# One attention-and-GLU kernel: its order of work planned with reserves, and one TensorE semaphore for two

## The chip, the core and the metric

The kernel runs on one core of one Trainium2 chip. The metric is the time of one execution on the device in microseconds (us), as the median of several runs. The core has five engines that take instructions in order from queues of their own and meet only through semaphores: TensorE (PE in the profile; its weight loads are PEld), VectorE (DVE), ScalarE (ACT), GpSimd (POOL) and SyncE (SP, which here only issues DMAs).

## The reference

`x` has 2048 tokens of 512 features, in bf16. The result mixes two branches by a gate per token:

```python
g = sigmoid((x * gate_w).sum(-1, keepdims=True))
qkv = x @ wqkv                      # 32 heads of 16
p = softmax(q @ k.T / 4)            # per head, 2048 x 2048
a = (p @ v) @ wo
b = ((x @ w_gate) * (x @ w_up)) @ w_down      # 1376 hidden
out = g * a + (1 - g) * b
```

## The kernel before

**The attention.** 32 heads in 4 stretches of 512 queries are handled as 32 *quads*: a quad is four heads (one of 8 sets) for one stretch `c` of queries (`quad`, line 187). For a quad the keys come in 16 tiles of 128; one key tile of one quad is a *step*, so there are 512 steps. A step has four score products of 128 keys by 512 queries, each into one PSUM bank. The exponential of the four banks is taken in one of two ways:

- an A step by ScalarE: `exp` (line 1709) reads one bank, or two neighbouring banks at once, and writes bf16 cells in whatever buffers are free (PT, and hT, wd, wu, wg, wo, xT while they aren't needed for themselves);
- a D step by VectorE: `dpass` (line 1747) adds a constant, clips, and writes int16 whose bits are an approximate exponential. `copy` (line 1756), on VectorE or GpSimd, makes three shifted copies, so that TensorE can sum four approximations (buffers DB, wv, wk). Only key tiles 2, 4, 7, 9, 12 and 14 may be D steps; whichever of them the planner doesn't give to VectorE falls to ScalarE.

Then V products add up the quad's output in PSUM bank 7. When the 16 steps of a quad are in, `o_copy` (line 1828) takes it out and its softmax sums go through DRAM for the division.

**The fill.** All other products (K, Q, V, gate, up, down, output projection) are *units* of a list that `setup` writes; a unit takes one bank, and VectorE empties it.

**The two halves.** TensorE is used as two halves of 64 rows, `r` = 0 and 1. `pe64` (line 1616) issues one product as four matmuls on four column groups of one half; a unit runs its first part in one half and the second in the other. Seven PSUM banks (0 to 6) are shared among A products, D products and fill.

**What sets the order.** Nothing is in loops: `_Sched` plays the kernel through on the host, before it is built, with durations for each engine, and every decision of this play writes the next instruction of an engine's queue. So its durations and thresholds decide only the order of the instructions on each engine; on the chip each waits for what it needs. The lines that matter:

- `s_a` (line 305) and `s_d` (line 333) issue a score product for ScalarE or VectorE and note when it is ready for it: `t = self.now + 0.385 + 0.056`.
- `try_act` counts an exponential as 0.833 ns a column and 0.051 us; the bank is free 0.12 + 0.05 us after that. `dve_pass` counts a pass as 0.065 us and 0.533 us a bank, and 0.083 us more to its end.
- `try_pe` and `pe_phase` choose the next product. The thresholds are tables in `PAR`, one value for each of 180 windows of 4 us of planned time, written as (count, value). Among them: `alook`, `alook2` (exponential products that may stand unread), `amax`, `dmax`, `fmax` (banks of A, D and fill), `skew` (lead of one half), `dact` (open D steps), `dl` (most D steps of a quad), `dend` (with fewer steps left than this in the current quad, no more D steps of it), `fstart` (units in their first part), `ghalf`, `gfull` (VectorE's backlog from which GpSimd takes copies), `cpmax`.

**Waits.** `_Plan.op` gives each operation a *stream*, which is one semaphore; products of half `r` have stream `pe0` or `pe1`. `_Plan.emit` (line 48) leaves out a wait that the engine knows to be met already, by an earlier wait on the same stream or by what the awaited operation itself had waited for; products of the same half don't wait for each other, since TensorE runs in order. For each stream that is left the greatest count is waited for by a `wait_ge` (line 82). An instruction carries one wait; a further one is an instruction of its own on the queue, which the profile has under L82.

Of the kernel before, what the change touches and what calls it, by code (L numbers as in the profile page):

```python
# [15 lines left out]
class _Op:  # L16
    __slots__ = ("eng", "fn", "deps", "stream", "inc", "seq", "count", "waits", "needed", "know")

    def __init__(self, eng, fn, deps, stream, inc):
        self.eng = eng  # L20
        self.fn = fn
        self.deps = deps
        self.stream = stream
        self.inc = inc
        self.seq = 0
        self.count = 0
        self.waits = []
# [109 lines left out]
class _Sched:  # L137
# [167 lines left out]
    def s_a(self, r):  # L305
# [20 lines left out]
        t = self.now + 0.385 + 0.056  # L326
# [6 lines left out]
    def s_d(self, r):  # L333
# [22 lines left out]
        t = self.now + 0.385 + 0.056  # L356
# [363 lines left out]
    def try_act(self):  # L720
# [51 lines left out]
        dur = 0.833e-3 * 512 * n + 0.051  # L772
# [10 lines left out]
        t = self.now + dur + 0.12 + 0.05  # L783
# [75 lines left out]
    def dve_pass(self, now):  # L859
# [9 lines left out]
        if self.dready and self.dready[0][0] <= now and (mate or not hold):  # L869
# [12 lines left out]
            dur = 0.065 + 0.533 * n  # L882
# [4 lines left out]
            t = self.now + dur + 0.083  # L887
# [661 lines left out]
class _Hw:  # L1549
# [66 lines left out]
    def pe64(self, r, mms, deps):  # L1616
        def fn(pe):
            o = None
            for dst, lhs, rhs, st, sp, cc in mms:
                o = pe.matmul(dst, lhs, rhs, start=st, stop=sp, tile_position=(64 * r, 32 * cc), skip_group_check=True)  # L1620
            return o

        return self.P.op("pe", fn, deps, "pe%d" % r)
# [302 lines left out]
    def prologue(self):  # L1926
# [119 lines left out]
        if self.par["acc"]:  # L2046
# [14 lines left out]
 'alook': ((13, 2), (5, 6), (8, 4), (6, 2), (9, 4), (3, 5), (21, 2), (3, 3), (3, 2), (1, 4), (5, 2), (18, 5),  # L2061
# [4 lines left out]
 'amax': ((7, 5), (35, 4), (6, 5), (81, 4), (6, 5), (45, 4)),  # L2066
 'amin': ((7, 3), (6, 2), (13, 4), (6, 2), (9, 3), (3, 2), (6, 4), (2, 2), (22, 3), (28, 4), (5, 3), (18, 4),
          (7, 3), (5, 4), (5, 2), (19, 4), (5, 3), (5, 4), (9, 3)),
 'apick': ((38, 0), (6, 1), (3, 0), (6, 1), (2, 0), (2, 1), (4, 0), (12, 1), (1, 0), (12, 1), (5, 0), (1, 1),
           (5, 0), (14, 1), (11, 0), (25, 1), (14, 0), (6, 1), (13, 0)),  # L2070
 'ares': ((5, 1), (6, 2), (3, 1), (21, 2), (3, 1), (6, 2), (7, 1), (1, 2), (8, 1), (17, 2), (15, 1), (6, 0),
          (24, 2), (9, 1), (9, 0), (22, 2), (18, 1)),
 'await': ((2, 0.05), (10, 0), (6, 0.05), (5, 0), (6, 0.2), (3, 0), (3, 0.2), (3, 0.1), (3, 0.2), (3, 0),
           (7, 0.05), (1, 0.2), (8, 0.05), (11, 0), (3, 0.2), (6, 0), (3, 0.4), (6, 0.05), (3, 0.1), (10, 0),
           (5, 0.4), (4, 0.2), (10, 0.05), (1, 0.4), (3, 0), (15, 0.05), (2, 0.2), (19, 0.05), (3, 0.4),
           (8, 0), (8, 0.2)),
 'cpmax': ((2, 10), (9, 6), (24, 8), (3, 5), (6, 8), (11, 2), (5, 3), (11, 6), (1, 5), (10, 10), (17, 14),
           (3, 2), (19, 8), (1, 14), (5, 6), (6, 14), (2, 10), (5, 5), (22, 8), (12, 3), (6, 8)),
 'dact': ((13, 2), (13, 3), (18, 2), (16, 3), (12, 2), (30, 3), (19, 2), (4, 3), (22, 2), (14, 3), (1, 2),
          (12, 3), (6, 2)),  # L2080
 'dahead': ((7, 0), (34, 1), (14, 0), (35, 1), (3, 0), (4, 1), (5, 0), (59, 1), (10, 0), (9, 1)),
# [13 lines left out]
 'dpair': ((17, 1), (6, 2), (3, 0), (15, 1), (14, 0), (13, 1), (6, 2), (9, 0), (4, 2), (7, 0), (1, 2), (2, 1),  # L2095
           (5, 2), (9, 0), (10, 1), (10, 0), (6, 1), (10, 0), (18, 1), (1, 0), (14, 1)),
 'dpri': ((13, 1), (31, 0), (20, 1), (1, 0), (6, 1), (26, 0), (5, 1), (40, 0), (5, 1), (25, 0), (8, 1)),
 'dresv': ((67, 0), (7, 1), (7, 2), (99, 0)),
 'dwait': ((2, 0.4), (11, 0), (5, 0.2), (5, 0.4), (3, 0.1), (12, 0.2), (6, 0), (7, 0.2), (1, 0), (8, 0.2),
           (11, 0.4), (3, 0.2), (9, 0.4), (6, 0.2), (8, 0.1), (14, 0), (10, 0.2), (21, 0.4), (5, 0),  # L2100
           (14, 0.2), (6, 0.1), (3, 0), (1, 0.1), (9, 0)),
 'fcf': ((7, 1), (34, 0), (3, 1), (136, 0)),
 'fdebt': ((2, 0), (12, -10), (12, 25), (6, -30), (9, 0), (1, -30), (6, 0), (12, -10), (5, 25), (6, -30),
           (3, 0), (9, 25), (3, 10), (9, 0), (7, 25), (9, 0), (10, 10), (8, 25), (6, 0), (2, 10), (5, -10),
           (5, 10), (14, 25), (5, 0), (1, 10), (3, -10), (10, 10)),
 'ffn0': 2.6,
 'ffn1': 31.5,
 'flead': ((2, 160), (3, 0), (15, 80), (3, 160), (15, 80), (6, 160), (7, 20), (1, 160), (8, 20), (2, 80),
           (9, 10), (6, 80), (15, 160), (10, 10), (5, 40), (4, 160), (18, 80), (5, 20), (3, 0), (3, 20),
           (7, 160), (14, 80), (13, 40), (6, 80)),  # L2110
 'fmax': ((18, 3), (8, 2), (18, 3), (6, 2), (21, 1), (12, 2), (9, 3), (10, 1), (19, 3), (1, 2), (5, 3),
          (10, 2), (43, 3)),
 'fres': ((44, 0), (16, 2), (29, 0), (13, 2), (28, 0), (2, 2), (10, 1), (38, 0)),
 'fs2': ((13, 1), (22, 0), (3, 1), (6, 0), (20, 1), (10, 0), (6, 1), (3, 0), (6, 1), (3, 0), (9, 1), (20, 0),
         (4, 1), (10, 0), (5, 1), (22, 0), (18, 1)),
# [108 lines left out]
```

## Time and profile before

| what | value |
|---|---|
| median of 3 runs | 709.44 us (707.34 to 713.36) |
| profiled execution | 708.04 us; its span, first to last instruction, 706.3 us |
| granted TensorE clock | 1.00 |
| SyncE's DMA queue, q1 | 18.86 MB, 11.1% of the 16 DMA engines |
| HBM | 11.71 MB read, 2.36 MB written |

A row of the groups reads: line, engine, operation, output<-input by the names of the buffers, shapes, count, then busy us and mean ns of one, then the idle time of the engine ahead of these instructions and what ended it. A row of the waits reads: engine, what it was about to write, line, what it waited for, then us in total, times, and the longest. In a row of a line's own view three durations stand for the least, the median and the greatest in ns. Only waits of 0.15 us and more are listed; shorter gaps count as the pipeline's own. PEld's rows stand for TensorE's queue, since a product starts with its weight load.

### The profile page before, as it was taken

The numbers are of one execution on the slowest core, as the hardware profiler recorded it, in microseconds if no ns is written. First come the engines' busy times: TensorE is split into PE (matmuls) and PEld (weight loads), VectorE is DVE, ScalarE is ACT, GpSimd is POOL, SyncE is SP. The second block draws the span as 40 slices with busy tenths as digits, with TensorE's granted clock in tenths as the row PEclk, the third lists the DMA queues.
The fourth block names the chain that finished last, engine by engine and source line by source line (L and its number), as shares of the span: only waits on it lengthen the run. The fifth ranks groups of instructions, "written<-read, shape, count | busy, mean of one in ns | idle before, by whom it ended". The sixth has DMA issues, their size and how long they took to land.

```text
span 706.3 us, 47734 instructions
## 1 busy us (share of the span) xinstructions
PE 692.3 (98%) x22103; PEld 358.7 (51%) x22103; DVE 645.9 (91%) x1060; ACT 684.8 (97%) x820; POOL 450.7 (64%) x351
## 2 busy tenths in 40 slices
PE   8999999999999999999999999999999999999997
PEld 4564555554444545554554445555553555555553
DVE  5999999899999999999998998999999978989985
ACT  6899999999999999999999999999999999999994
POOL 3365658877464666655675747777666788487630
PEclk9999999999999999999999999999999999999999
DMA  9202341003010100001000010100001010000101
GB/s 156 69 6 57 78 107 36 6 20 94 16 35 5 35 18 23 28 11 28 13 23 23 15 33 19 36 13 13 27 7 40 12 36 24 14 23 18 29 19 33
DMA packets 33752, 22.97 MB, mean 33 GB/s; under 512 B 19500, under 2 KB 30156, under 8 KB 33552
## 3 DMA queue, kind: packets, MB, share of 16 engines
q1 hardware_dynamic: 32416, 18.86, 11.1%
q8 instruction: 173, 2.83, 1.6%
q0 software_dynamic: 176, 0.53, 0.3%
q10 hardware_dynamic: 960, 0.52, 0.3%
q14 instruction: 27, 0.22, 0.1%
HBM read 11.71 MB, written 2.36 MB: 20 GB/s over the span
## 4 chain that ended last, share of the span: by engine, by line
PE 90%; DVE 3%; ACT 3%; issue 1%; DMA 1%; ACTq 0%; DVEq 0%
PE ps L1620 90%; DVE DB L1754 2%; ACT xT L1718 1%; ACT PT L1718 1%; DVE DB L1760 1%; DMA DB<-in_A_x_dram 1%; ACT wu L1718 0%; DVE wv L1754 0%; DVE oc L1830 0%; DVE hT L1902 0%; PE ps L2017 0%; ACTq L1933 0%; DVE wu L1813 0%; ACT wd L1718 0%; ACT QM L2030 0%
## 5 line engine op out<-in xcount | busy, mean ns | idle before, releaser
L1620 PE MATMUL ps<-QM,KT 64*32 64x512 bf16 x8192 | 496.6, 379 | 4.2 <-issue 1.3
L1764 POOL TENSOR_TENSOR DB<-DB,cadd 128x512 int32<-128x512 int32 (+1 forms) x207 | 280.2, 1373 | 146.9 <-DVE DB L1760 62.0
L1718 ACT ACTIVATE PT<-ps 128x1024 bf16<-128x1024 f32 (+1 forms) x394 | 358.5, 1016 | 1.6 <-PE ps L1620 0.7
L1754 DVE TENSOR_SCALAR DB<-ps 128x512 int16<-128x512 f32 (+1 forms) x493 | 327.7, 692 | 31.8 <-PE ps L1620 28.3
L1620 PE MATMUL ps<-DB,Vs 64*17 64x512 bf16 x2856 | 261.6, 377 | 0.7
L1718 ACT ACTIVATE xT<-ps 128x1024 bf16<-128x1024 f32 (+1 forms) x270 | 258.6, 1043 | 1.9 <-PE ps L1620 1.7
L1620 PEld LDWEIGHTS ps<-QM,KT 64*32 64x32 bf16 x8192 | 152.2, 89 | 177.9 <-ACT PT L1718 46.9
L1620 PE MATMUL ps<-PT,Vp 64*17 64x512 bf16 x1444 | 204.5, 376 | 0.3 <-issue 0.2
L1620 PE MATMUL ps<-xT,Vp 64*17 64x512 bf16 x1030 | 165.3, 376 | 0.2
L1620 PE MATMUL ps<-xT,wu 64*32 64x512 bf16 x1376 | 111.9, 377 | 0.0
L1620 PE MATMUL ps<-xT,wg 64*32 64x512 bf16 x1376 | 110.5, 377 | 1.0 <-issue 0.9
L1760 DVE TENSOR_SCALAR DB<-DB 128x2048 int16<-128x2048 int16 (+1 forms) x160 | 107.3, 701 | 0.6 <-PE ps L1620 0.2
L1620 PE MATMUL ps<-wd,hT 64*32 64x512 bf16 x1408 | 100.2, 377 | 0.1
L1620 PE MATMUL ps<-DB,Vp 64*17 64x512 bf16 x1000 | 97.0, 377 | 0.6 <-DVE oc L1830 0.2
L1620 PEld LDWEIGHTS ps<-DB,Vs 64*17 64x17 bf16 x2856 | 70.6, 87 | 37.0 <-PE ps L1620 10.5
L1718 ACT ACTIVATE wd<-ps 128x1024 bf16<-128x1024 f32 (+1 forms) x69 | 65.7, 1059 | 0.6 <-PE ps L1620 0.4
L1764 POOL TENSOR_TENSOR DB<-wv,cadd 128x512 int32<-128x512 int32 (+1 forms) x38 | 49.7, 1331 | 24.2 <-DVE wv L1754 9.6
L1620 PEld LDWEIGHTS ps<-PT,Vp 64*17 64x17 bf16 x1444 | 51.2, 87 | 17.9 <-PE ps L1620 4.6
L1764 POOL TENSOR_TENSOR wv<-DB,cadd 128x512 int32<-128x512 int32 (+1 forms) x31 | 42.1, 1371 | 19.7 <-DVE DB L1760 7.8
L1754 DVE TENSOR_SCALAR wv<-ps 128x512 int16<-128x512 f32 x72 | 47.6, 683 | 2.5 <-PE ps L1620 2.1
L1764 POOL TENSOR_TENSOR wk<-DB,cadd 128x512 int32<-128x512 int32 (+1 forms) x30 | 39.4, 1324 | 15.8 <-DVE DB L1760 11.2
L1620 PEld LDWEIGHTS ps<-xT,Vp 64*17 64x17 bf16 x1030 | 40.8, 87 | 11.6 <-PE ps L1620 2.6
(108 smaller groups left out, 839.5 us busy)
## 6 DMA issues: line engine op xcount, KB each, us to landing
rb<-rscr SPq DMA_DIRECT2D x16, 256.0 KB
QM<-qraw SPq DMA_DIRECT2D x124, 16.0 KB, 2.3
oc<-oraw SPq DMA_DIRECT2D x60, 32.0 KB, 2.2
out_dram<-ost SPq DMA_DIRECT2D x12, 128.0 KB, 1.7
wd<-in_B_w_down_dram SPq DMA_DIRECT2D x10, 128.0 KB, 2.5
wu<-in_B_w_up_dram SPq DMA_DIRECT2D x12, 96.0 KB, 2.2
wg<-in_B_w_gate_dram SPq DMA_DIRECT2D x12, 96.0 KB, 2.6
wv<-in_A_wqkv_dram POOLq DMA_DIRECT2D x1, 512.0 KB, 5.2
```

The source lines that it names most:

```text
L1620: o = pe.matmul(dst, lhs, rhs, start=st, stop=sp, tile_position=(64 * r, 32 * cc), skip_group_check=True)
L1718: return self.P.op("act", lambda a: a.activation(dst, src, ACT.Exp, scale=self.ES), deps)
L1754: return self.dve(lambda v: v.tensor_scalar(dst, src, self.YB, 0.0, ALU.add, ALU.max), deps)
L1760: return self.dve(lambda e: e.tensor_scalar(o, a, 32.0 * v, None, ALU.add), deps)
L1764: lambda e: e.tensor_tensor(o.bitcast(I32), a.bitcast(I32), self.cadd[:, v, :].bitcast(I32).to_broadcast([128, n]), ALU.add),
```

## The change

1. Each operation of TensorE by `pe64` goes to one stream, `pe`, so both halves count on one semaphore. A new field `half` keeps what was left out before: products of the same half don't wait for each other.
2. The planner counts a score product as ready later, by 0.09 us for ScalarE (`mga`) and by 0.06 us for VectorE (`mgd`).
3. The planner's fixed parts move: ScalarE 0.051 to 0.055 us (and 0.12 to 0.116 after it), VectorE 0.065 to 0.069 (and 0.083 to 0.079 after it).
4. The tables of thresholds in `PAR` are other ones, 36 of them, and with them the order of the work on all engines. Formats, sizes, buffers, the computation and the number of D key tiles allowed stay.

The diff, cut to its core; of the tables those that the prediction names:

```diff
 class _Op:
-    __slots__ = ("eng", "fn", "deps", "stream", "inc", "seq", "count", "waits", "needed", "know")
+    __slots__ = ("eng", "fn", "deps", "stream", "inc", "seq", "count", "waits", "needed", "know", "half")
...
+        self.half = None
...
-                if d.eng == "pe" and o.eng == "pe" and d.stream == o.stream:
+                if d.eng == "pe" and o.eng == "pe" and d.half == o.half:
                     continue
...
-        t = self.now + 0.385 + 0.056
+        t = self.now + 0.385 + 0.056 + self.par["mga"]
         self.cnt += 1
         heapq.heappush(self.aready, (t, self.cnt, e, ci, bank, op))
...
-        t = self.now + 0.385 + 0.056
+        t = self.now + 0.385 + 0.056 + self.par["mgd"]
         self.cnt += 1
         heapq.heappush(self.dready, (t, self.cnt, e, ci, bank, op))
...
-        dur = 0.833e-3 * 512 * n + 0.051
+        dur = 0.833e-3 * 512 * n + 0.055
...
-        t = self.now + dur + 0.12 + 0.05
+        t = self.now + dur + 0.116 + 0.05
...
-            dur = 0.065 + 0.533 * n
+            dur = 0.069 + 0.533 * n
...
-            t = self.now + dur + 0.083
+            t = self.now + dur + 0.079
...
-        return self.P.op("pe", fn, deps, "pe%d" % r)
+        o = self.P.op("pe", fn, deps)
+        o.half = r
+        return o
...
- 'alook2': ((18, 4), (5, 3), (9, 0), (6, 2), (3, 0), (3, 3), (3, 0), (5, 5), (1, 3), (2, 0), (5, 6), (11, 3),
-            (3, 5), (9, 3), (6, 2), (6, 6), (6, 5), (1, 4), (29, 0), (4, 6), (5, 2), (7, 0), (10, 4), (10, 0),
-            (13, 4)),
- 'amax': ((7, 5), (35, 4), (6, 5), (81, 4), (6, 5), (45, 4)),
+ 'alook2': ((8, 4), (5, 3), (1, 4), (3, 6), (1, 4), (5, 3), (9, 0), (5, 5), (21, 4), (10, 6), (10, 4), (2, 3),
+            (3, 0), (8, 4), (1, 6), (3, 5), (9, 6), (6, 4), (18, 5), (21, 4), (6, 5), (9, 0), (16, 6)),
+ 'amax': ((7, 5), (157, 4), (6, 5), (10, 4)),
...
- 'dact': ((13, 2), (13, 3), (18, 2), (16, 3), (12, 2), (30, 3), (19, 2), (4, 3), (22, 2), (14, 3), (1, 2),
-          (12, 3), (6, 2)),
+ 'dact': ((13, 2), (24, 3), (4, 2), (3, 3), (14, 2), (79, 3), (8, 2), (19, 3), (6, 1), (10, 3)),
...
- 'dend': ((2, 2), (3, 3), (2, 1), (10, 0), (6, 3), (1, 4), (2, 1), (11, 4), (7, 3), (6, 2), (21, 3), (6, 4),
-          (3, 0), (7, 4), (2, 2), (3, 4), (10, 0), (9, 4), (10, 2), (1, 3), (15, 1), (5, 3), (5, 2), (14, 0),
-          (1, 4), (12, 3), (6, 2)),
+ 'dend': ((2, 2), (3, 3), (2, 1), (10, 0), (20, 3), (4, 5), (3, 0), (6, 2), (18, 4), (3, 3), (4, 4), (3, 3),
+          (2, 0), (12, 4), (3, 0), (15, 2), (3, 5), (6, 3), (3, 5), (3, 0), (3, 3), (12, 2), (3, 3), (9, 4),
+          (6, 3), (6, 4), (6, 2), (10, 4)),
...
- 'dmax': ((5, 2), (18, 3), (3, 2), (15, 3), (14, 2), (16, 3), (3, 2), (3, 3), (3, 2), (3, 3), (7, 2), (8, 3),
-          (4, 2), (9, 3), (29, 2), (2, 3), (5, 2), (19, 3), (1, 2), (3, 1), (10, 2)),
+ 'dmax': ((5, 2), (3, 3), (24, 2), (12, 3), (6, 2), (30, 3), (3, 2), (8, 3), (10, 2), (79, 3)),
...
- 'fmax': ((18, 3), (8, 2), (18, 3), (6, 2), (21, 1), (12, 2), (9, 3), (10, 1), (19, 3), (1, 2), (5, 3),
-          (10, 2), (43, 3)),
+ 'fmax': ((41, 3), (17, 1), (8, 2), (5, 3), (9, 2), (3, 3), (8, 2), (19, 1), (18, 3), (14, 1), (11, 2),
+          (11, 3), (6, 1), (10, 2)),
...
- 'fstart': ((20, 2), (6, 1), (1, 2), (15, 1), (18, 2), (2, 1), (9, 2), (3, 1), (13, 2), (7, 1), (39, 2),
-            (4, 1), (43, 2)),
+ 'fstart': ((11, 2), (6, 1), (3, 2), (15, 1), (6, 2), (30, 1), (4, 2), (3, 1), (2, 2), (3, 1), (8, 2),
+            (22, 1), (6, 2), (29, 1), (1, 2), (9, 1), (12, 2), (10, 1)),
...
- 'ghalf': ((7, 0.7), (1, 0.5), (17, 1.2), (1, 0.7), (15, 0.5), (3, 0.9), (3, 0.3), (5, 1.2), (1, 0.9),
-           (14, 0.3), (5, 0.7), (6, 0.5), (5, 0.7), (19, 0.3), (19, 0.5), (8, 0.7), (5, 0.5), (6, 9),
-           (7, 0.5), (10, 1.2), (8, 0.3), (2, 0.5), (13, 1.2)),
+ 'ghalf': ((7, 0.7), (1, 0.5), (6, 1.2), (15, 0.5), (3, 0.9), (9, 0.5), (18, 0.3), (5, 0.5), (1, 0.3),
+           (3, 0.5), (12, 1.2), (3, 0.5), (8, 1.2), (19, 0.3), (3, 0.5), (12, 0.9), (3, 0.5), (12, 0.3),
+           (3, 0.5), (3, 1.2), (9, 0.9), (6, 0.5), (3, 0.3), (6, 0.7), (10, 0.5)),
...
+ 'mga': 0.09,
+ 'mgd': 0.06,
...
- 'skew': ((18, 3), (5, 2), (12, 4), (3, 2), (3, 4), (6, 2), (15, 3), (5, 2), (14, 6), (1, 2), (5, 4), (3, 3),
-          (2, 1), (10, 3), (19, 1), (8, 2), (3, 6), (4, 4), (4, 6), (7, 1), (14, 3), (6, 1), (13, 2)),
+ 'skew': ((2, 3), (16, 4), (5, 2), (9, 4), (5, 6), (4, 4), (3, 3), (14, 6), (1, 1), (3, 3), (6, 1), (3, 4),
+          (7, 3), (2, 6), (3, 2), (3, 3), (6, 4), (15, 3), (3, 4), (18, 6), (12, 4), (9, 3), (12, 6), (3, 4),
+          (3, 3), (3, 4), (10, 3)),
```

More of the change, by code (lines that the diff above doesn't have):

```diff
@@ L2102 @@
[L2102 to L2105, printed above, removed]
+ 'alook': ((13, 2), (5, 6), (8, 4), (6, 2), (9, 6), (6, 2), (3, 4), (8, 2), (2, 6), (2, 5), (3, 6), (6, 5),
+           (4, 2), (3, 5), (15, 2), (3, 6), (5, 2), (7, 6), (2, 2), (15, 6), (3, 3), (24, 2), (12, 6), (6, 2),
+           (10, 5)),
@@ new lines @@
+ 'apick': ((11, 0), (17, 1), (52, 0), (3, 1), (6, 0), (17, 1), (55, 0), (3, 1), (16, 0)),
+ 'ares': ((14, 1), (9, 2), (9, 1), (5, 2), (1, 1), (3, 2), (3, 0), (14, 1), (10, 0), (10, 2), (2, 1), (11, 2),
+          (13, 1), (6, 0), (15, 2), (15, 0), (15, 2), (15, 1), (10, 0)),
+ 'await': ((2, 0.05), (10, 0), (6, 0.05), (5, 0), (3, 0.2), (6, 0.1), (5, 0.2), (1, 0), (3, 0.05), (3, 0),
+           (12, 0.05), (2, 0), (1, 0.1), (3, 0.4), (6, 0), (10, 0.05), (2, 0), (3, 0.2), (6, 0.05), (5, 0.1),
+           (16, 0), (18, 0.2), (12, 0), (6, 0.05), (3, 0.2), (9, 0.05), (6, 0.4), (6, 0.2), (10, 0.4)),
@@ new lines @@
+ 'dpair': ((8, 1), (3, 2), (17, 0), (1, 1), (3, 2), (9, 0), (27, 1), (3, 2), (9, 0), (3, 1), (11, 0), (1, 2),
+           (15, 1), (15, 0), (3, 2), (12, 1), (18, 0), (6, 2), (16, 1)),
+ 'dpri': ((21, 1), (29, 0), (9, 1), (105, 0), (6, 1), (10, 0)),
+ 'dresv': ((8, 0), (5, 3), (79, 0), (9, 1), (79, 0)),
+ 'dwait': ((2, 0.4), (3, 0), (20, 0.2), (1, 0.1), (6, 0.2), (5, 0.4), (1, 0.2), (3, 0), (3, 0.1), (11, 0),
+           (10, 0.1), (3, 0.4), (9, 0.2), (3, 0.1), (11, 0.2), (4, 0), (15, 0.1), (18, 0.4), (9, 0.1),
+           (9, 0.2), (6, 0.1), (6, 0), (6, 0.4), (6, 0), (10, 0.1)),
@@ L2140 @@
  'ov': [[], [], [], []],
- 'pfirst': ((22, 0), (4, 1), (12, 0), (33, 1), (3, 0), (28, 1), (5, 0), (12, 1), (2, 0), (9, 1), (32, 0),
-            (10, 1), (8, 0)),
+ 'pfirst': ((22, 0), (1, 1), (6, 0), (3, 1), (5, 0), (28, 1), (18, 0), (8, 1), (1, 0), (18, 1), (18, 0),
+            (3, 1), (39, 0), (10, 1)),
  'ph': 1,
```

76 lines of the change are left out of this document (35 added, 41 removed), and 17 rows, old and new, of the table PAR.

## The prediction

> **What bounds the kernel now.** I read the page's engine shares first, then its chain, then the stretches of time, and then the waits of the engines that came out nearly full.
>
> ```profile
> span 706.3 us, 47734 instructions
> PE 692.3 (98%) x22103; PEld 358.7 (51%) x22103; DVE 645.9 (91%) x1060; ACT 684.8 (97%) x820; POOL 450.7 (64%) x351
> PE 90%; DVE 3%; ACT 3%; issue 1%; DMA 1%; ACTq 0%; DVEq 0%
> ```
>
> PE's 98% is no bound by itself: matmuls overlap, so its busy time says little. ACT's 97% means more, since ACT does one thing at a time. The stretches show where it holds (the columns are PE, PEld, DVE, ACT and POOL busy, with counts).
>
> ```profile
> core 0: us, PE busy (x) PEld busy (x) DVE busy (x) ACT busy (x) POOL busy (x), PEclk, DMA share, GB/s
> 300.00:340.00 40.00, 39.96 (x1356) 20.94 (x1344) 38.52 (x64) 39.96 (x44) 22.73 (x23) 1.00 0.08 21
> ...
> 40.00:690.00 650.00, 644.30 (x20755) 332.73 (x20747) 606.54 (x981) 646.04 (x756) 434.35 (x331) 1.00 0.11 28
> ```
>
> In the 650 us between 40 and 690 us ACT is idle for 4.0 us, DVE for 43.5 us. The granted clock is 1.00, so nothing can come from there. Next the waits.
>
> ```profile
> PEld ps L1620 <- ACT PT L1718: 47.4, 187, 0.8
> PEld ps L1620 <- ACT xT L1718: 35.3, 131, 0.8
> PEld ps L1620 <- DVE DB L1754: 31.7, 130, 0.6
> DVE DB L1754 <- PE ps L1620: 28.3, 76, 1.7
> ```
>
> TensorE waits 82.7 us for ScalarE to hand back PSUM banks (first two rows), and VectorE waits 28.3 us for score products. So **ScalarE's exponentials bound the steady part**; TensorE, the one on the chain, mostly passes ScalarE's pace on.
>
> **How much time ScalarE really loses.** Its busy time contains pipeline overlap, so I count slots. Two rows of ACT's timeline with pairs of banks (1024 columns), and one with single banks:
>
> ```profile
> 301.57 1.96 ACT L1718 ACTIVATE PT<-ps 128x1024 bf16<-128x1024 f32 x2
> 303.38 1.07 ACT L1718 ACTIVATE xT<-ps 128x1024 bf16<-128x1024 f32 x1
> ...
> 35.04 4.09 ACT L1718 ACTIVATE wu<-ps 128x512 bf16<-128x512 f32 x8
> ```
>
> From 301.57 to 303.38 are two starts, 0.905 us each: a pair holds ACT for 0.905 us though its record lasts 1.08. Eight single banks last 4.09 us; less the last one's 0.62 (the mean of the wd group with 512 columns) that is 3.47/7 = 0.50 us a single. The counts:
>
> ```profile
> L1718 ACT ACTIVATE PT<-ps 128x1024 bf16<-128x1024 f32 x328 | 326.8, 1087 | 0.9 <-PE ps L1620 0.2
> L1718 ACT ACTIVATE xT<-ps 128x1024 bf16<-128x1024 f32 x245 | 244.0, 1082 | 1.9 <-PE ps L1620 1.7
> L1718 ACT ACTIVATE wd<-ps 128x1024 bf16<-128x1024 f32 x66 | 63.9, 1079 | 0.6 <-PE ps L1620 0.4
> L1718 ACT ACTIVATE wu<-ps 128x1024 bf16<-128x1024 f32 x5 | 4.9, 1027 | 0.1
> L1718 ACT ACTIVATE hT<-ps 128x1024 bf16<-128x1024 f32 x4 | 4.5, 1118 | 0.0
> L1718 ACT ACTIVATE wd<-ps 128x512 bf16<-128x512 f32 x3 | 1.9, 621 | 0.0
> ...
> 0.00:706.30 706.30, 677.88 (x807) 1.00 0.13 33
> ...
> L1718 ACT ACTIVATE xT<-ps x270: 591/1070/1283, 169.6 to 694.4; 128x1024 bf16<-128x1024 f32 x122, 128x512 bf16<-128x512 f32 x13
> L1718 ACT ACTIVATE wu<-ps x26: 572/625/1056, 9.1 to 48.9; 128x512 bf16<-128x512 f32 x21, 128x1024 bf16<-128x1024 f32 x5
>   PE ps L1620: 6.1, 12
> ```
>
> 328 + 245 + 66 + 5 + 4 = 648 pairs of 807 exponentials leave 159 others. Slots: 648 x 0.905 + 159 x 0.50 = 586.4 + 79.5 = 665.9 us. The first starts at 9.1, the last at 694.4 and takes a slot: about 685.8 us. So 19.9 us are lost, of them 1.0 for two gate exponentials that are no part of the 807. The last row (idle time ahead of L1718) puts 6.1 us down to 12 long waits for products; the other 12.8 us are gaps under 0.15 us, which that view leaves out.
>
> Here a figure of the Trainium skill speaks against any gain: "ScalarE: Activation LUTs", section "What ACT_TABLE_LOAD costs", gives 186 ns plus 0.833 ns an element with 93 ns of overlap, which by estimate is 0.946 us a pair and would leave ScalarE no lost time, so that the term for the reserve below would be 0. The trace disagrees with 0.905.
>
> **The change part by part.**
>
> *One semaphore.* Before, TensorE's two row halves count on two semaphores, and an instruction that needs both waits twice; the second wait is an instruction of its own at L82.
>
> ```profile
> L82 ACTq EVENT_SEMAPHORE  x622: 17/17/17, 3.8 to 694.3; - x156
> L82 PEldq EVENT_SEMAPHORE  x55: 51/51/51, 3.8 to 700.1; - x55
> ```
>
> Most of ACT's 622 should go. On the path they would cost 622 x 0.017 = 10.6 us, the best end. But 622 waits for 807 exponentials means that most of the pairs at 0.905 us have one ahead of them; ACT's queue clears it while the exponential before still runs. I take **0**. That cover is gone only where ACT is late, 12 times by the row above: 0.2 us. The worst end is that a common count makes someone wait longer; it is a rival below. On POOL (64% busy, so its waits are covered) and PE's queue (55 x 0.051 = 2.8 us at most, mostly waits for DMAs, which stay) I take 0 too.
>
> *The reserve for ScalarE (mga 0.09 us).* The planner now counts a score product as ready for ScalarE 0.09 us later, so an order that it calls tight has the product done 0.09 us ahead. Gaps shorter than that can close, long ones shrink by 0.09. Bounds: 0, and 12.8 + 12 x 0.09 = 13.9 us. Beside it the tables let more exponential products stand in PSUM (mean over the 180 windows of the diff: alook2 2.5 to 4.1, skew 2.9 to 4.1) and start fewer other products at once (fstart 1.8 to 1.3, fmax 2.5 to 2.1), which points the same way. A part of the 12.8 us is jitter that no order removes, and the nearer row is the 12 long waits, which mostly stay. I take **5.5 us**, 0.4 of the upper end.
>
> *The reserve for VectorE (mgd 0.06 us).*
>
> ```profile
> L1754 DVE TENSOR_SCALAR DB<-ps 128x512 int16<-128x512 f32 x486 | 319.5, 685 | 30.3 <-PE ps L1620 26.8
> L1754 DVE TENSOR_SCALAR wv<-ps 128x512 int16<-128x512 f32 x72 | 47.6, 683 | 2.5 <-PE ps L1620 2.1
> L1754 DVE TENSOR_SCALAR wk<-ps 128x512 int16<-128x512 f32 x20 | 13.0, 683 | 0.7 <-PE ps L1620 0.6
> L1754 DVE TENSOR_SCALAR DB<-ps 128x1024 int16<-128x1024 f32 x7 | 8.5, 1218 | 1.5 <-PE ps L1620 1.5
>   PE ps L1620: 31.0, 85
> ...
> 255.97 2.47 DVE L1754 TENSOR_SCALAR DB<-ps 128x512 int16<-128x512 f32 x4
> 258.36 0.68 DVE L1786 TENSOR_SCALAR qraw<-ps 128x512 bf16<-128x512 f32 x1
> ...
> 0.00:706.30 706.30, 152.16 (x234) 1.00 0.13 33
> ```
>
> 486 + 72 + 20 + 2 x 7 = 592 banks went to VectorE, four to a step: 148 of the 512 steps; ScalarE did 364. Four passes take 258.36 - 255.97 = 2.39 us. The last row is L1760, VectorE's copies of those results: 234 instructions, 152.16/148 = 1.03 us a step at most. So a step costs VectorE some 3.4 us and saves ScalarE two pairs, 1.81 us. The waits for products, 31.0 us in 85, shrink by at most 85 x 0.06 = 5.1 us, or 1.5 steps, 2.7 us of ScalarE; at least by 0, if no step moves, because VectorE is not the bound. I take about half, **1.5 us**.
>
> *True distances and the rest.* 0.051 to 0.055 (ACT) and 0.065 to 0.069 (DVE) in the planner move nothing on the chip by themselves; the sums to a bank's release stay equal (0.12 to 0.116, 0.083 to 0.079). Instruction kinds, sizes and DMA bytes stay; DMAs are reordered with the work that produces them, and the mean DMA share of 0.11 between 40 and 690 us covers that. POOL takes copies sooner (ghalf 0.95 to 0.62): it has 36% free, and what it takes frees VectorE, which has room. 0 each. If this cover is gone, a late copy holds back a V product.
>
> *Sum.* 0 - 5.5 - 1.5 = -7.0 us. The profiled execution took 708.04 us (span 706.3 and 1.7 around it), so 701.0; the median of the three runs, 709.44, is 1.4 above it: **702.4 us**. Late next is the same engine, ScalarE, at 0.905 us a pair.
>
> **The rivals.**
>
> *A: VectorE takes more steps.* If the order feeds it so that most of the 31.0 us are used, 31.0/3.4 = 9 steps move, 16.3 us off ScalarE; with 5.5 us kept: 709.4 - 21.8 = 687.6, half of it 698. For it: VectorE's 43.5 idle us, dact 2.5 to 2.7 and dmax 2.5 to 2.7. Against: dend rises 2.2 to 2.8, which hands a quad's last steps to ScalarE, and TensorE pays for more V products.
>
> *B: nothing to gain.* The gaps are jitter and the new order fills ScalarE as well as the old: 709 within 3 us. For it: 4.0 idle us out of 650.
>
> *C, slower: waiting exponential products starve VectorE of banks.* Place: PSUM's seven shared banks. A bank with an unread product for ScalarE is no bank for VectorE's, and TensorE stops in order at the next product without one (31.7 us after DVE's banks, 82.7 after ACT's now). With alook2 at 4.1 that grows; VectorE's 28.3 us grow, steps fall back to ScalarE at 1.81 us each. Once 4 steps more fall back than the reserve's 5.5 us pays for (3 to break even, 7 in all for over 1% slower) it decides: 10 steps give 709.4 + 18.1 - 5.5 = 722.0. Against: amax stays at 4.1, and fmax falls.
>
> *D: the second waits are on the path*, 10.6 us: 698.8 alone. Against it the 0.905 us with them.
>
> *E: the halves finish out of step,* and one count makes a reader of one half wait for the other's earlier product: up to a matmul's 0.377 us (the page's mean) at ACT's 12 waits and DVE's 85, 4.5 us on ACT's path and 32 us on DVE, or 9 steps, 16 us: up to 730.
>
> ```profile
> L1620 PE MATMUL ps<-DB,Vs 64*17 64x512 bf16 x2856 | 261.6, 377 | 0.7
> ```
>
> For E the Trainium skill says in "TensorEngine Tiling (Array Packing)", section "Key Properties", that tiles operate independently. Against E it says in "TensorE: Matmul & The Clock Gate", section "Part 3: Packing small matmuls — row/col tiling", that matmuls start and end in program order. The ends in this trace are modelled, so no run here shows it.
>
> **How the numbers follow.** Forecast (4 to 12 us less) 0.40; A 0.12; B 0.18; C 0.24; D 0.03; E 0.03. A measurement here tells about 1%, 7.1 us, from no change. Beyond it on the fast side: half the forecast (0.20), A and D: 0.35. On the slow side: two thirds of C and of E: 0.18. Within: 0.47. The time is the forecast's, 702.4, its own range 697 to 706. The range that leaves out no more than 2 in 10 cuts half of A and less than half of C and E: 692 to 719.
>
> **What would show it.** Semaphore: L82 on ACT well under 622, pairs still 0.905 us apart. Reserve for ScalarE: slots as counted above, lost time near 14 us, long waits fewer than 12. Reserve for VectorE: under 31.0 us in 85 waits, 592 banks or a few more. Wrong would be: fewer banks on VectorE (C), over 610 (A), lost time still near 20 (B), or ScalarE's start after a product later than before (E).

## The result, and the profile after

| kernel | runs | median, us | lowest to highest, us |
|---|---|---|---|
| before | 20 | 709.92 | 705.85 to 713.36 |
| after | 20 | 705.92 | 702.39 to 709.00 |

After stands to before at 0.9933, 95% interval 0.9918 to 0.9948: 4.0 us or 0.7% less, a small gain, but the interval leaves out 1. Forecast were 702.4 us and 1% faster, in a range of 692 to 719. The profiled execution of after took 703.74 us, 4.3 us less than that of before. In the changed kernel all lines behind 82 stand one to three further down: the wait is L83, TensorE's products L1621, the exponential L1721, VectorE's pass L1757.

From the page of after, its span, the engine shares and the chain:

```profile
span 702.0 us, 47197 instructions
PE 688.9 (98%) x22151; PEld 370.6 (53%) x22151; DVE 652.3 (93%) x1063; ACT 681.2 (97%) x839; POOL 460.4 (66%) x328
PE 71%; ACT 26%; DVE 1%; DMA 1%; issue 0%; ACTq 0%; DVEq 0%
```

The shares are nearly those of before. ScalarE carries 26% of the chain instead of 3%, but that tells nothing of the gain. These are the chains of two runs that come below, sem_only (before's order, as slow as before) and order_two_sem (after's order, as fast as after):

```profile
PE 60%; ACT 34%; DVE 4%; issue 1%; DMA 1%; ACTq 0%; DVEq 0%
...
PE 94%; ACT 2%; DVE 1%; issue 1%; DMA 1%; ACTq 0%; DVEq 0%
```

ScalarE's share is 34% in the slower kernel and 2% in the faster one, so this share doesn't follow the time. The same stretch as before, 40 to 690 us, from the windows:

```profile
40.00:690.00 650.00, 645.65 (x20980) 346.98 (x20964) 616.56 (x990) 647.16 (x781) 443.72 (x308) 1.00 0.11 28
```

ScalarE is idle for 2.8 us there instead of 4.0, VectorE for 33.4 instead of 43.5. TensorE issues 225 matmuls more in the stretch, VectorE 9 instructions more and ScalarE 25 more. The waits of after:

```profile
PEld ps L1621 <- ACT PT L1721: 51.7, 207, 0.8
PEld ps L1621 <- PE ps L1621: 29.2, 89, 0.6
PEld ps L1621 <- ACT xT L1721: 26.9, 112, 0.5
DVE DB L1757 <- PE ps L1621: 16.7, 55, 0.8
PEld ps L1621 <- DVE DB L1757: 16.0, 70, 0.6
PEld ps L1621 <- issue: 10.3, 26, 1.7
```

What changed clearly is on VectorE's side: it waits 16.7 us for its score products instead of 28.3, and TensorE waits 16.0 us for VectorE's banks instead of 31.7. TensorE's wait for ScalarE's banks is 78.6 us in these two rows, against 82.7. The time fell by 4.3 us while these waits fell by 31.4, so most of them were not time of the kernel. "issue" is time in which TensorE's queue waits for nothing that the profile shows; before it was

```profile
PEld ps L1620 <- issue: 13.7, 31, 1.6
```

The exponentials of after, from the groups by shape, the window of that line alone, and the line's own view:

```profile
L1721 ACT ACTIVATE PT<-ps 128x1024 bf16<-128x1024 f32 x370 | 365.5, 1116 | 1.8 <-PE ps L1621 1.8
L1721 ACT ACTIVATE xT<-ps 128x1024 bf16<-128x1024 f32 x179 | 183.4, 1110 | 0.7 <-PE ps L1621 0.6
L1721 ACT ACTIVATE wd<-ps 128x1024 bf16<-128x1024 f32 x60 | 59.2, 1127 | 0.0
...
L1721 ACT ACTIVATE wu<-ps 128x1024 bf16<-128x1024 f32 x7 | 7.0, 1028 | 0.0
L1721 ACT ACTIVATE hT<-ps 128x1024 bf16<-128x1024 f32 x4 | 4.1, 1036 | 0.0
...
L1721 ACT ACTIVATE wg<-ps 128x1024 bf16<-128x1024 f32 x2 | 2.2, 1125 | 0.0
```

```profile
0.00:702.10 702.10, 674.16 (x826) 1.00 0.13 33
```

```profile
L1721 ACT ACTIVATE xT<-ps x232: 592/1080/1301, 214.9 to 691.3; 128x1024 bf16<-128x1024 f32 x87, 128x512 bf16<-128x512 f32 x29
...
L1721 ACT ACTIVATE wu<-ps x25: 574/685/1058, 9.6 to 52.1; 128x512 bf16<-128x512 f32 x18, 128x1024 bf16<-128x1024 f32 x7
...
  PE ps L1621: 6.9, 16
```

Counted as the prediction counts: 370 + 179 + 60 + 7 + 4 + 2 = 622 pairs and 204 singles, against 648 and 159. Slots 622 x 0.905 + 204 x 0.50 = 664.9 us. The first starts at 9.6, the last at 691.3 and takes a slot: 682.2 us, of which 17.3 are lost, against 19.9. But this count is off in two places. In before, one pair (the first row here) was counted as a single, and the last exponential (the second row) is a pair:

```profile
L1718 ACT ACTIVATE wg<-ps 128x1024 bf16<-128x1024 f32 x1 | 1.0, 1024 | 0.1
...
694.38 1.02 ACT L1718 ACTIVATE xT<-ps 128x1024 bf16<-128x1024 f32 x1
```

So before has 649 pairs and 158 singles, together the 1456 banks of its 364 steps. And a single holds ScalarE for 0.477 us, not 0.50: that is the median time from the start of a single to the next start in after (0.478 in before), as it is 0.904 us for a pair in both. The eight singles from which the prediction took its 0.50 came a little late each. Counted again with 0.904 and 0.477:

| us | before | after |
|---|---|---|
| until the first exponential | 9.1 | 9.6 |
| slots | 662.1 | 659.6 |
| lost between the slots | 24.2 | 22.6 |
| behind the last slot | 11.0 | 10.2 |

The long waits for products are 16 with 6.9 us, not fewer than 12 with 6.1; sem_only, with before's order, has 23 with 8.1, so this row differs between executions as much as between the orders. VectorE's passes by shape, and the row of its waits in the line's own view:

```profile
L1757 DVE TENSOR_SCALAR DB<-ps 128x512 int16<-128x512 f32 x450 | 296.5, 686 | 20.8 <-PE ps L1621 15.8 <-POOL DB L1767 0.5
...
L1757 DVE TENSOR_SCALAR wv<-ps 128x512 int16<-128x512 f32 x76 | 50.4, 686 | 2.1 <-PE ps L1621 1.4
L1757 DVE TENSOR_SCALAR wk<-ps 128x512 int16<-128x512 f32 x56 | 36.8, 684 | 1.5 <-PE ps L1621 1.2
...
L1757 DVE TENSOR_SCALAR DB<-ps 128x1024 int16<-128x1024 f32 x7 | 8.5, 1219 | 1.0 <-PE ps L1621 0.8
L1757 DVE TENSOR_SCALAR wv<-ps 128x1024 int16<-128x1024 f32 x2 | 2.4, 1223 | 0.3 <-PE ps L1621 0.3
```

```profile
  PE ps L1621: 19.6, 66
```

450 + 76 + 56 + 2 x 9 = 600 banks, 150 D steps: two more than before. The waits for products fell from 31.0 us in 85 to 19.6 in 66. And the waits that are instructions of their own:

```profile
L83 PEldq EVENT_SEMAPHORE  x52: 51/51/450, 3.7 to 689.7; - x52
...
L83 ACTq EVENT_SEMAPHORE  x1: 17/17/17, 3.8 to 3.8; - x1
```

ScalarE's 622 second waits are gone but for one.

**Where the 4.3 us of the profiled spans lie,** by ScalarE's account in that table: slots -2.5, lost time -1.6, the part behind the last exponential -0.8, and +0.5 for the later start. The slots hide two movements. Two D steps more on VectorE take four pairs off ScalarE, 3.6 us. But 23 of the remaining pairs were issued as two singles, at 0.954 instead of 0.904 us: 1.15 us back. Two more pairs of runs below have these two orders, and the same count gives nearly the same for them: slots -2.5 both times, lost time 27.3 to 25.7 us (sem_only to order_two_sem) and 19.3 to 17.6 (vq_before to vq_after).

### The profile page after: what moved, and what is told of

Its sections match the earlier page's. It is cut to its first block, busy times and chain, and to the rows that moved or that the text cites. A ratio compares the mean times of both kernels' runs of the same rounds, so it can differ in the third digit from the quotient of the medians.

```text
span 702.0 us, 47197 instructions
## 1 busy us (share of the span) xinstructions
PE 688.9 (98%) x22151; PEld 370.6 (53%) x22151; DVE 652.3 (93%) x1063; ACT 681.2 (97%) x839; POOL 460.4 (66%) x328
## 3 DMA queue, kind: packets, MB, share of 16 engines
q8 instruction: 173, 2.83, 1.7%
## 4 chain that ended last, share of the span: by engine, by line
PE 71%; ACT 26%; DVE 1%; DMA 1%; issue 0%; ACTq 0%; DVEq 0%
PE ps L1621 70%; ACT PT L1721 16%; ACT xT L1721 8%; ACT wd L1721 2%; DMA DB<-in_A_x_dram 1%; ACT wu L1721 1%; DVE DB L1757 0%; DVE hT L1905 0%; ACT wg L1721 0%; PE ps L2020 0%; DVE oraw L1833 0%; DVE wv L1757 0%; ACTq L1936 0%; ACT QM L2033 0%; DVEq L88 0%
## 5 line engine op out<-in xcount | busy, mean ns | idle before, releaser
L1621 PE MATMUL ps<-QM,KT 64*32 64x512 bf16 x8192 | 497.2, 379 | 3.4 <-ACT wd L1721 0.8
L1721 ACT ACTIVATE PT<-ps 128x1024 bf16<-128x1024 f32 (+1 forms) x449 | 404.3, 1049 | 1.8 <-PE ps L1621 1.8
L1767 POOL TENSOR_TENSOR DB<-DB,cadd 128x1024 int32<-128x1024 int32 (+1 forms) x186 | 279.0, 1519 | 141.5 <-DVE DB L1763 56.2
L1757 DVE TENSOR_SCALAR DB<-ps 128x512 int16<-128x512 f32 (+1 forms) x457 | 304.8, 694 | 21.8 <-PE ps L1621 16.7
L1621 PE MATMUL ps<-DB,Vs 64*17 64x512 bf16 x3024 | 275.6, 377 | 0.5 <-issue 0.3
L1621 PEld LDWEIGHTS ps<-QM,KT 64*32 64x32 bf16 x8192 | 155.0, 90 | 162.5 <-ACT PT L1721 51.1
L1621 PE MATMUL ps<-PT,Vp 64*17 64x512 bf16 x1638 | 227.5, 377 | 0.2
L1721 ACT ACTIVATE xT<-ps 128x1024 bf16<-128x1024 f32 (+1 forms) x232 | 211.4, 1028 | 0.9 <-PE ps L1621 0.8
L1621 PE MATMUL ps<-xT,Vp 64*17 64x512 bf16 x822 | 145.9, 377 | 0.1
L1621 PE MATMUL ps<-xT,wu 64*32 64x512 bf16 x1376 | 110.5, 377 | 0.0
L1621 PE MATMUL ps<-xT,wg 64*32 64x512 bf16 x1376 | 108.2, 377 | 0.0
L1621 PE MATMUL ps<-wd,hT 64*32 64x512 bf16 x1408 | 102.2, 377 | 0.0
L1621 PEld LDWEIGHTS ps<-DB,Vs 64*17 64x17 bf16 x3024 | 74.1, 87 | 34.0 <-PE ps L1621 5.1
L1621 PE MATMUL ps<-DB,Vp 64*17 64x512 bf16 x928 | 89.7, 377 | 0.8 <-DVE oraw L1833 0.3
L1621 PEld LDWEIGHTS ps<-PT,Vp 64*17 64x17 bf16 x1638 | 56.6, 87 | 21.0 <-PE ps L1621 7.2
L1721 ACT ACTIVATE wd<-ps 128x1024 bf16<-128x1024 f32 (+1 forms) x73 | 66.1, 1058 | 0.0
L1757 DVE TENSOR_SCALAR wv<-ps 128x512 int16<-128x512 f32 (+1 forms) x78 | 52.7, 699 | 2.5 <-PE ps L1621 1.7
L1621 PEld LDWEIGHTS ps<-wd,hT 64*32 64x32 bf16 x1408 | 36.8, 92 | 13.0 <-issue 1.2
L1621 PEld LDWEIGHTS ps<-xT,wu 64*32 64x32 bf16 x1376 | 35.5, 92 | 13.3 <-DVE DB L1757 1.0
L1621 PEld LDWEIGHTS ps<-xT,wg 64*32 64x32 bf16 x1376 | 34.8, 92 | 13.5 <-DVE DB L1757 1.3
```

Source lines behind the costliest of these rows:

```text
L1721: return self.P.op("act", lambda a: a.activation(dst, src, ACT.Exp, scale=self.ES), deps)
L1757: return self.dve(lambda v: v.tensor_scalar(dst, src, self.YB, 0.0, ALU.add, ALU.max), deps)
L1767: lambda e: e.tensor_tensor(o.bitcast(I32), a.bitcast(I32), self.cadd[:, v, :].bitcast(I32).to_broadcast([128, n]), ALU.add),
```

## The experiments

All ratios are to the kernel before, run beside each experiment on the same chip; its median there was 706.5 to 712.6 us, so times from different chips are compared by their ratios. The first question was which part gains: the semaphore or the order. Then, what in the order: that products come earlier for ScalarE (the theory of the prediction), that VectorE keeps up better, or the reserve as such. And how hard ScalarE binds.

### The semaphore alone, and the order alone

sem_only is before with this edit and nothing else:

```diff
-                if d.eng == "pe" and o.eng == "pe" and d.stream == o.stream:
+                if d.eng == "pe" and o.eng == "pe" and d.half == o.half:
...
-        return self.P.op("pe", fn, deps, "pe%d" % r)
+        o = self.P.op("pe", fn, deps)
+        o.half = r
+        return o
```

> The order of before, instruction for instruction, with one semaphore for both halves of TensorE. Theory 1 (the second waits are hidden behind the exponential before them): L82's waits on ACT fall from 622 to a few, pairs stay 0.905 us apart, ratio to before 1.000 within 0.003. Theory 2 (the waits are on ScalarE's path): up to 10.6 us less, ratio 0.985 to 0.997. Theory 3 (one count makes readers of one half wait for the other): ratio 1.005 or more, and the 6.1 us of ScalarE's long waits and the 31.0 us of VectorE's grow.

Measured: 712.56 us, 1.0018 (0.9994 to 1.0043). Rows of its waits and of the line of waits:

```profile
PEld ps L1621 <- DVE DB L1757: 31.0, 126, 0.6
DVE DB L1757 <- PE ps L1621: 30.9, 79, 1.7
...
PEld ps L1621 <- issue: 21.0, 49, 0.8
```

```profile
L83 ACTq EVENT_SEMAPHORE  x1: 17/17/17, 3.8 to 3.8; - x1
```

621 instructions of ScalarE's queue are gone and nothing is won: the 10.6 us of rival D don't come. Nor is there a loss as in E, up to the 0.4% that the interval leaves, and VectorE waits nearly as it did (30.9 us in 79, against 28.3 in 76).

order_two_sem is after with the old stream put back:

```diff
-        o = self.P.op("pe", fn, deps)
+        o = self.P.op("pe", fn, deps, "pe%d" % r)
         o.half = r
```

> The order of after with the two semaphores of before. Theory 1: the same time as after, ratio to before 0.993 within 0.003, so the whole gain is the order's. Theory 2: the gain of 0.67% is in good part the semaphore's, and this kernel falls back to a ratio of 0.997 to 1.000, with some 600 waits on ACT back under the line of the wait.

Measured: 706.43 us, 0.9939 (0.9915 to 0.9963), as after. The line of waits, and three pairs in a row of ScalarE's timeline:

```profile
L83 ACTq EVENT_SEMAPHORE  x593: 17/17/17, 3.8 to 692.7; - x198
```

```profile
302.63 2.85 ACT L1721 ACTIVATE PT<-ps 128x1024 bf16<-128x1024 f32 x3
305.34 0.63 ACT L1721 ACTIVATE xT<-ps 128x512 bf16<-128x512 f32 x1
```

With 593 second waits in the queue the pairs start (305.34 - 302.63)/3 = 0.903 us apart; in after, without them, it is the same:

```profile
301.34 2.86 ACT L1721 ACTIVATE PT<-ps 128x1024 bf16<-128x1024 f32 x3
304.05 0.64 ACT L1721 ACTIVATE xT<-ps 128x512 bf16<-128x512 f32 x1
```

So the gain is the order's, within these intervals, and a second wait on ScalarE's queue lies beside the exponential before it.

### The time in which TensorE waits for nothing

With before's order, TensorE stood 13.7 us at a span of 706.3 and 21.0 us at 709.9 (sem_only). So I asked whether the orders differ only in how TensorE's instructions arrive. vq_before and vq_after cut TensorE's matmuls and weight loads by 12%, by leaving out three of the four matmuls of each V product of a shifted copy:

```diff
         mms = []
-        for cc in range(4):
+        for cc in range(4 if v == 0 else 1):
```

> The order and semaphores of before, with a part of the computation left out: of each V product of a shifted copy (v = 1 to 3) only the first of its four matmuls is issued, 2664 matmuls and their weight loads fewer (12% of TensorE's instructions). The order of the products, their slots on TensorE and all waits stay. Theory F (TensorE runs out of instructions: its idle time put down to issue, 13.7 us in 31 waits in before and 21.0 in 49 with one semaphore, in spans of 706.3 and 709.9, is the fetch of instructions in blocks of 16 KB, and every product behind it comes late): the issue waits fall to 3 us or less and the time by 8 to 12 us, ratio 0.983 to 0.989. Theory R (late products come from waits a little longer than planned, which the reserves cover; the fetch is hidden): ratio 0.998 to 1.002.

> The order and semaphore of after with the same matmuls left out (150 steps on VectorE, 2700 matmuls). Theory F: the issue waits, 10.3 us in 26, fall to 3 us or less, the time falls by 5 to 8 us, ratio to before 0.983 to 0.987, and the two orders come within 0.3% of each other: then the new order was faster because it ran out of instructions less. Theory R: ratio 0.993 as for after, and the 0.7% between the two orders stays.

Measured: 703.28 us, 0.9901 (0.9875 to 0.9927), and 698.44 us, 0.9836 (0.9808 to 0.9864). TensorE in vq_before, from the page, and the row of its waits; then the same of vq_after:

```profile
PE 688.2 (98%) x19439; PEld 356.3 (51%) x19439; DVE 646.7 (92%) x1060; ACT 682.3 (97%) x820; POOL 450.6 (64%) x351
```

```profile
PEld ps L1620 <- issue: 2.0, 4, 0.7
```

```profile
PEld ps L1621 <- issue: 0.5, 2, 0.3
```

The stalls go (13.7 to 2.0 us, 10.3 to 0.5), each order gains about 7 us, and the spread goes with them: six runs lie within 2.2 us (702.18 to 704.38) and 1.7 us (698.03 to 699.68), where eleven of before beside them spread over 6.5. For before, 7 us is less than the 8 to 12 of theory F, and far from the unchanged time of theory R. But both orders gain alike: 0.9836/0.9901 = 0.9934 is the ratio of after to before. The stalls cost both and are not the difference. What these two runs don't separate is the stall from the work of the matmuls that were left out.

### The reserve in the search

Three kernels are after with tables that I searched anew, all with the same short search, for three settings of the reserve. The 36 tables differ between them; the settings are

```diff
- 'mga': 0.09,
- 'mgd': 0.06,
+ 'mga': 0.0,
+ 'mgd': 0.0,
```

for res_none, 0.09 and 0.06 unchanged for res_same, and 0.20 and 0.15 for res_large. In the planner's own play, the first two end within 0.3 us of each other.

> After with both reserves 0 and tables searched anew for that, by a short search of our own (the same procedure and effort for this kernel and the next two). In the planner's own play this order and the next one end equally, within 0.3 us. Theory R (the reserves make the chip follow the plan more closely): this kernel is slower than the next one by 4 to 6 us, the difference that is left between before and after when TensorE never runs out of instructions. Theory S (the searched tables are merely another sample, the reserves do nothing): the two kernels agree within 2 us. Against before itself this order is worse by the shorter search, ratio 1.00 to 1.02.

> After with its reserves of 0.09 and 0.06 us and tables of our own short search; in the planner's play it ends with the order of the run before, within 0.3 us. Theory R: 4 to 6 us faster than that one, ratio to before about 1.000 to 1.008. Theory S: within 2 us of it.

> Reserves of 0.20 and 0.15 us, tables of our own short search by the same effort; the planner's play ends 13.5 us later than with 0.09 and 0.06, since the reserves count as time there. Theory R with a saturating effect: the chip gives back some 3 to 5 us of these 13.5, so this kernel is 8 to 11 us slower than the one with 0.09 and 0.06. If the reserve goes on paying in full, the two agree within 4 us. Theory S: 13 us slower or more.

| kernel | mga, mgd, us | median, us | ratio (95%) |
|---|---|---|---|
| res_none | 0, 0 | 713.16 | 1.0014 (0.9991 to 1.0036) |
| res_same | 0.09, 0.06 | 715.14 | 1.0044 (1.0020 to 1.0067) |
| res_large | 0.20, 0.15 | 725.54 | 1.0193 (1.0157 to 1.0229) |

The reserve of 0.09 did not help: its point value has the wrong sign for the theory that planning with a reserve makes the order faster on the chip. One order for each setting is little, and res_same with after's settings lies 1.1% above after (1.0044 against 0.9933), so what the search finds matters more than the setting. What a reserve is worth at an equally deep search stays open.

res_large took 10.4 us more than res_same where the planner's play ends 13.5 later, which is the 8 to 11 us expected if the chip gives back a part of a larger reserve. But the plays themselves speak against the reserve as the reason. By what `_Sched.run` returns on the host they end at 688.2 us for before, 689.3 for after, 698.65 for res_none, 698.97 for res_same and 712.5 for res_large. So the gain of after is not in its plan, which is 1.1 us longer than that of before: the chip took 21.7 us more than planned for before (709.92) and 16.6 for after (705.92). On the chip of this table it took 24.4 us more than planned for before (712.63), and 14.5, 16.2 and 13.0 for the three. An order found with no reserve at all thus keeps to its plan some 10 us better than before's. The longer fixed part in the planner (0.004 us on each of some 800 exponentials) can account for about 3 of these; what makes the rest isn't shown.

### Products one place earlier

A direct trial of "products come earlier": in the finished order, each score product whose bank had been free for 0.1 us of planned time is moved one place ahead on TensorE, past the product before it (1077 products in early_before, 1133 in early_after). Work and counts are the same.

```diff
+    def mark(self, op, bank):
+        if op is not None and self.now > 40.0 and self.now - self.bput[bank] >= 0.1:
+            self.hw.P.early.append(op)
...
+            x = ops[i]
+            if x in self.early or x in o.deps or x.stream == "pex":
+                continue
+            if any(ops.index(d) > i for d in o.deps):
+                continue
+            del ops[j]
+            ops.insert(i, o)
```

> The order of before with a reserve put into it by hand: after 40 us of planned time each score product whose bank had been free for 0.10 us or more is issued one product earlier on TensorE (1077 of 2048 products, 751 of them for ScalarE); nothing else moves. Theory R (products that reach ScalarE and VectorE earlier are what the new order gains): 3 to 6 us less than before, ratio 0.991 to 0.996, VectorE's waits for products (31.0 us in 85) clearly lower. Theory S (the gain is another mix of work, not the lead of the products): within 2 us, ratio 0.997 to 1.003. If V products or fill that come one place later are what ends last: slower by 2 us or more.

> The same by hand on the order of after (1133 products moved ahead by one). Theory R with reserves already in: within 2 us of after, ratio to before 0.991 to 0.996. Theory S: the same, so this run only tells how much lead is still to be had; below 0.990 would mean that reserves larger than those planned pay.

Measured: 720.77 us, 1.0198 (1.0177 to 1.0219), and 712.77 us, 1.0084 (1.0065 to 1.0104), which is 1.5% above after. Waits of early_before, whose lines stand 31 further down than in before:

```profile
PEld ps L1651 <- PE ps L1651: 44.0, 114, 0.6
...
DVE DB L1785 <- PE ps L1651: 33.3, 84, 2.6
...
PEld ps L1651 <- issue: 5.5, 12, 2.1
```

TensorE's wait for its own products grew from 29.0 us in 91 (before) to 44.0 in 114, and VectorE's waits grew too, from 28.3 us to 33.3. A product moved ahead pushes back the one it passes; that this one was due as well fits these waits, but was not tried by itself. An earlier product is thus no gain by itself.

### How hard ScalarE and VectorE bind

exp496 is after with all exponentials on 496 of the 512 columns, and the columns left out are set to zero once at the start. Work of ScalarE shrinks, and the order stays.

```diff
-            dst = t[:, i : cells[1][1] + 1 : s, :]
-            src = self.ps[:, banks[0] : banks[1] + 1, :]
+            dst = t[:, i : cells[1][1] + 1 : s, 0:496]
+            src = self.ps[:, banks[0] : banks[1] + 1, 0:496]
```

> After with a part of the computation left out: every exponential on ScalarE reads and writes 496 of 512 columns of a bank (the other columns of the cells stay 0 or old). By the slots (0.904 us for 1024 columns and 0.477 for 512, so 0.834 ns a column) 622 pairs and 204 singles shrink by 19.3 us in all; every order and wait stays. Theory B (ScalarE bounds the whole way): 15 to 19 us less than after, ratio to before 0.966 to 0.972. Theory P (the planned order is tight on all engines at once, and a faster ScalarE only waits for products): 0 to 8 us less, ratio 0.982 to 0.993.

Measured: 696.22 us, 0.9845 (0.9825 to 0.9866). Its timeline and its waits:

```profile
298.04 2.77 ACT L1721 ACTIVATE PT<-ps 128x992 bf16<-128x992 f32 x3
300.68 0.61 ACT L1721 ACTIVATE xT<-ps 128x496 bf16<-128x496 f32 x1
301.14 0.62 ACT L1721 ACTIVATE PT<-ps 128x496 bf16<-128x496 f32 x1
```

```profile
PEld ps L1621 <- PE ps L1621: 35.3, 109, 0.6
PEld ps L1621 <- DVE DB L1757: 22.0, 98, 0.5
...
PEld ps L1621 <- ACT PT L1721: 15.0, 64, 0.5
```

A pair now holds ScalarE for 0.880 us instead of 0.903. Over 622 pairs that is 14 us, with the singles (half of it, 204 times) 17 us; by the planner's 0.833 ns a column it is 19.3 us. The time fell by 0.9933 - 0.9845 = 0.0088 of 707 us, 6.2 us (4 to 8 by the two intervals): about **a third**, inside the 0 to 8 us of theory P. The rest came back as gaps: counted with 0.880 us a pair and 0.464 a single, ScalarE's lost time is 32.6 us instead of 22.6. TensorE's wait for PT's exponentials went from 51.7 to 15.0 us, while its waits for itself and for VectorE grew by 12.1. So with this order ScalarE binds only in part. That TensorE is next, almost at once, is what these waits suggest; it was not tried by itself.

dve496_before and dve496_after do the same to VectorE: its passes of the D steps take 496 columns.

```diff
-            dst = self.db[buf].rearrange("p (a b) -> p a b", b=512)[:, lo : hi + 1 : hi - lo, :]
-            src = self.ps[:, i : i + 2, :]
+            dst = self.db[buf].rearrange("p (a b) -> p a b", b=512)[:, lo : hi + 1 : hi - lo, 0:496]
+            src = self.ps[:, i : i + 2, 0:496]
```

> The order and semaphores of before, with a part of the computation left out: each pass of VectorE over a bank of scores does 496 of 512 columns (592 banks, 16 columns each at 1.04 ns by the slots 1.131 and 0.598 us for two banks and one: 9.9 us of VectorE in all). ScalarE, all products, waits and the order stay. Theory V (in before it is the passing to and fro between TensorE and VectorE that costs, 31.7 us of TensorE after VectorE's banks and 28.3 us of VectorE after products, and the new order gains by nearly halving both): 4 to 7 us less than before, ratio 0.990 to 0.994, near after's own 0.993. Theory B (only ScalarE's slots and gaps count): within 2 us of before.

> The same on the order of after (600 banks, 10.0 us of VectorE). Theory V: it gains clearly less than before's order does from the same, 0 to 3 us, ratio to before 0.989 to 0.993, and the two orders come closer. Theory B: within 2 us of after. A third way: both gain alike, 4 us or more, which leaves the 0.7% between them and speaks against V as the cause of the difference.

Measured: 706.91 us, 1.0007 (0.9992 to 1.0022), and 703.14 us, 0.9951 (0.9932 to 0.9969). Waits of dve496_before, then one of dve496_after:

```profile
PEld ps L1622 <- ACT PT L1720: 53.4, 206, 0.8
...
PEld ps L1622 <- DVE DB L1756: 26.1, 110, 1.2
```

```profile
PEld ps L1623 <- DVE DB L1759: 11.2, 51, 0.4
```

VectorE's banks come back sooner (31.7 to 26.1 us, 16.0 to 11.2), and the time doesn't move: the interval of dve496_before holds 1, and after's and dve496_after's overlap. What TensorE no longer waits for VectorE it waits for ScalarE (47.4 to 53.4 us in before's order). Theory V is out as it was put: 10 us less of VectorE's work gained nothing. These runs don't halve TensorE's waits for VectorE as the new order does, so that this most visible change of the profile made the kernel faster is unlikely by them, but not excluded.

## Why the prediction was right, and where it was wrong

The direction and the range held. The size was -4.0 us by the medians (-4.3 by the profiled executions) for a forecast of -7.0. That it came this near is in part luck: the largest term, four fifths of the forecast, measured 1.6 us of its 5.5, and others that were put lower or at 0 came in beside it.

- **One semaphore, 0:** right, by sem_only and order_two_sem, and with it the reason given (the second wait lies beside the exponential; pairs are 0.903 us apart with and without). D is out, and so is E but for the 0.4% that the interval leaves. For the order in which matmuls end, the prediction had the Trainium skill's "TensorE: Matmul & The Clock Gate", section "Part 3: Packing small matmuls — row/col tiling": program order. That one count for both halves costs nothing agrees with it.
- **The reserve for ScalarE, -5.5:** this term was mis-sized. Its base was misread: with 649 pairs and 0.477 us a single, lost time before was 24.2 us, not 19.9. It fell by 1.6 us, to 22.6, and the 14 us named as the sign are far off. Long waits did not become fewer (16 with 6.9 us). So the mechanism named for it, products done a little ahead, isn't seen in the profile; early_before and early_after show that putting products ahead by itself costs 1.5 to 2%, and res_none that a plan without a reserve is followed as well as one with it. What saved the 1.6 us is not settled.
- **The reserve for VectorE, -1.5:** waits fell by 11.4 us, twice the 5.1 named as the most, and two steps moved instead of 0.8: 3.6 us. The bound was wrong because it let only the reserve shrink the waits, while the whole order was new. Not in the sum was that 23 pairs split, 1.15 us, which leaves -2.5 us in the slots: by ScalarE's account this, and not the reserve for ScalarE, is the largest part.
- **The rest, 0:** -0.8 us behind the last exponential and +0.5 at the start were not foreseen.
- **The step beneath all terms failed:** "ScalarE's exponentials bound the steady part", with each of its microseconds counted as one of the kernel. exp496 gives 0.32 of a microsecond for one. What spoke for the bound, 4.0 idle us in 650 and TensorE's 82.7 us of waits for its banks, holds just as well when two engines are paced alike by an order that was planned to fit them. With 0.32 for one, the terms -5.5 and -1.5 would have given -2.2, too little this time. That points to part of the gain having come by another way than ScalarE's time, but the slope was measured on after's order alone.
- **Rival A** did not come (150 steps, not 157), and its price was too high by the same step. **B** was nearest among the rivals, and by its sign, lost time hardly lower, it was half right; but the interval leaves out 1, and the median lies at the slow end of the forecast's own 697 to 706. **C** is contradicted: TensorE's wait for VectorE's banks was halved, and steps moved to VectorE.

Shown: the gain is the order's and not the semaphore's, and it isn't TensorE's stalls without a wait (vq_after against vq_before). Made unlikely: VectorE's pace (dve496_before). Not shown: which of the 36 tables, the two reserves or the planner's fixed parts makes it. The account by ScalarE says where it sits, not why.

## What to carry to other kernels

Before a saving on a "97% busy" engine is counted in full, shave that engine a little with the order held and read the slope; here one microsecond of ScalarE was worth a third of one, and one of VectorE nothing. In an order planned to fit several engines, shorter waits can be worth nothing, and an issue moved one place ahead without planning the rest anew costs more than the planner's finest tuning brings. An extra wait instruction is priced by what it adds to the spacing of the work around it, not by its count: 593 of them left the pairs 0.903 us apart. And a wait view, a chain or a count of slots is worth reading on a second execution of the same order before a difference in it is explained.

## What the runs showed of the hardware

TensorE stands without any wait that the profile shows, up to 2.1 us at once (early_before). With before's order and all of its matmuls that was 13.7 us of a span of 706.3, 21.0 of 709.9 (sem_only) and 5.5 of 704.1 (dve496_before), so it differs between executions of one order. Instructions come by DMA queues of their own. The largest, in the pages of after and of vq_before:

```profile
q8 instruction: 173, 2.83, 1.7%
```

```profile
q8 instruction: 152, 2.49, 1.5%
```

2.83 MB in 173 packets is 16 KB a packet. It is also 64 bytes for each of after's 44302 matmuls and weight loads, as 2.49 MB is for the 38878 of vq_before, so this queue brings TensorE's instructions. 12% fewer matmuls and weight loads, and 21 packets fewer, all but ended the stalls, and the time fell by 7 us. That the stalls are late instructions is argued from this and was not tried by itself.

ScalarE's exponential from PSUM to bf16 starts every 0.904 us for 1024 columns and every 0.477 us for 512 (medians of after), and every 0.880 us for 992 in the three shown of exp496. The estimate of 0.946 us for 1024 columns, worked out from the Trainium skill's "ScalarE: Activation LUTs", section "What ACT_TABLE_LOAD costs", is above the 0.904 measured.
